# Linear attention and two expert layers in one kernel: the order of the stages, the shape of the attention products and the engine queues re-designed

## The chip, the cores and the metric

The kernel runs on one core of one Trainium2 chip. The metric is the device time of one execution in microseconds (us); the median of the runs before is 1416.45. The core has five engines with a queue each: TensorE (PE, matrix products; the loading of its stationary operand is listed apart as PEld), VectorE (DVE), ScalarE (ACT), GpSimd (POOL) and SyncE (SP, which here only issues transfers).

## The reference, cut to what matters

```python
def phi(x):                                   # q, k: (8 batches, 8 heads, 576 tokens, 64)
    proj = einsum('bhsd,df->bhsf', x, w_phi)  # 128 features
    proj = proj - max(abs(proj), axis=-1)
    return concatenate([exp(proj), exp(-proj)], -1)
q_p, k_p = phi(q), phi(k)
kv  = einsum('bhsf,bhsd->bhfd', k_p, v);  z = k_p.sum(2)
num = einsum('bhsf,bhfd->bhsd', q_p, kv)
den = einsum('bhsf,bhf->bhs', q_p, z)[..., None] + 1e-06
x = (num / den) -> (4608 tokens, 512)

h = x @ w_in                                  # 512 -> 1024; weights arrive as float64
e = exp(h - max(h));  solu = h * e / (sum(e) + 1e-9)
y = layernorm(solu) * g_ln @ w_out            # 1024 -> 512

logits = y @ w_gate + modality_bias[modality_id]   # 8 experts
e_idx = argmax(logits);  gate = softmax(logits)[e_idx]
out = gate * (relu(y @ w1[e_idx]) @ w2[e_idx])     # 512 -> 1024 -> 512
```

## The kernel before

The work has two parts. Class `P1` computes the attention and the first dense layer (`moe1`) for 36 tiles of 128 tokens and sends each token's place to a list of its expert. Class `P2` computes the chosen expert for slots of up to 256 tokens.

**Number formats.** Many products are made as three passes of a rounded format (`F32R`): high by high, high by low, low by high. The name ends in h or l. Where plain `F32` operands are multiplied, the trace shows two instructions, each with its own weight load, for one `matmul` of the code.

**The k side.** `k_fetch` brings one head's 512 rows (block of 64 x 512, twice on the 128 partitions; every ninth block holds the last 64 rows of all heads of a batch: 72 blocks). From block 18 on POOL splits a block into high and low halves. `k_phi` (L313) projects it, takes the largest magnitude of each row (DVE), and makes `exp(p-m)` and `exp(m-p)` on ACT in eight pieces of 128 columns, because the bias differs for each. `kv_head` (L363) multiplies the features of one head with `[v, 1]`: 8 products with 65 columns (16 instructions), two heads make a pair; `kM` adds the last 64 rows; `kE` copies the sums to `kvsb`, which holds two batches.

**The q side.** A unit `u` has 256 tokens of four heads (36 units). `q1` projects them transposed (feature on partition) into two PSUM banks that stay in use; DVE takes maxima over features by a transposing reduction; `q2` finishes them, splits them and sends them through two small transfers to two partitions (`mr`); `q3` subtracts them by one more product with `negones` and ACT makes the exponentials. `q_num` (L459) uses the q features as stationary operand, 128 tokens at a time:

```python
for sg in range(2):
    nc.tensor.matmul(o, qp[:, sg, h0 + h, tt*128:tt*128+128], kv[:, b % 2], start=(sg == 0), stop=(sg == 1))
```

Column 65 is the denominator; DVE divides. `x_T` turns each tile of x with four PE transposes and splits it.

**moe1.** `m_mm1` (L504) has 24 products of 512 columns, softmax and norm on ACT and DVE; `m_T` turns the result with 8 transposes; `m_mm2` (L556) has 48 products of 260 columns, the last 8 of which are the gate logits; `m_route` (L586) computes the place and POOL scatters it.

**The decoding of weights.** `prep_a` to `prep_e` turn 16 chunks of float64 weights into high and low parts, with passes over 128x512 elements on DVE, ACT and POOL, and 32 transposes and 32 small products on PE.

**The order.** All is interleaved: `PRO`, `LOOP`, `LOOP2`, `TAIL` are written-out lists of steps. `manual_schedule` fixes the order of PE (in `PRO` of SP too, in `TAIL` of POOL too); the other engines' orders are chosen by the planner.

```python
LOOP = "q3(u);lA(0);mT(t);kE();lA(1);num(u,0);q1(u+1);num(u,1);mm1(t+1);kV(0);kV(1);q2(u+1);mm2(t);xT(u);R(t-1);ql(u+2);kM()"
```

One round of `LOOP` handles one unit `u = t+4`, one tile `t` and one pair of heads of k; `LOOP2` is the same without k. `W(n)` in `PRO` are matmuls without use, 52 in all.

**The experts.** `star` picks the expert with most tokens so far and fetches its weights early; `T0`, `M1`, `M2` compute slot 0 while the last tiles are routed; `run` has the loop over further slots. The next expert's `w1` is split into high (ACT, `hi`) and low (DVE, `lo`) in four pieces after the present slot's first product, and PE waits (`sW`) for all four.

Of the kernel before, what the change touches and what calls it, by code (L numbers as in the profile page):

```python
# [17 lines left out]
KB = 2  # L18
QP = 512
KS = 4  # L20
KSBUF = 2
KRB = 3
KSB = 3
KOLD = 18
KAH = 2
VTB = 3
CWV = {0, 6, 13}
HV = {0, 3, 8, 9, 13, 14, 15}
HP_ = {4, 10, 13, 14}
QV = 4  # L30
LEAD = 4
HP = 1000
TF = 3
XB = 4
ENG = lambda E: {E.PE, E.SP}
PRO = """P();W(6);P();kA(0);P();kA(1);P();ql(1);P();kA(0);W(6);kV(0);kA(1);kV(1);P();kM();ql(0);kA(0);kV(0)
kE();kV(1);P();kA(1);kM();kA(0);P();kA(1);kV(0);q1(0);P();kV(1);W(14);q2(0);q1(1);kM();P();kV(0)
q3(0);P();kE();q2(1);kA(0);P();W(10);kA(1);kV(1);q3(1);P();kM();P();ql(2);kE();N(0);W(16);P();kE()
ql(3);P();kV(0);D(11);q1(2);kV(1);q2(2);P();D(8);kM();D(9);kA(0);P();F(8);P();kA(1);N(1);q1(3);kV(0)
D(12);q3(2);kV(1);kE();kM();P();q2(3);kA(0);kE();F(11);D(10);F(9);xT(1);kA(1);N(2);ql(4);B();q3(3)  # L40
kV(0);D(13);F(10);kV(1);q1(4);kM();N(3);ql(5);q2(4);kE();D(14);F(12);P();D(15);xT(3);F(14);kA(0)
q3(4);mm1(0);num(4,0);kA(1);kV(0);num(4,1);ql(6);F(13);q1(5);mT(0);F(15);kA(0);kV(1);q2(5);kM();q1(6)
kA(1);kE();mm2(0);kV(0);q3(5);mm1(1);R(0);q2(6);num(5,0);mm1(2);ql(7);kA(0);kV(1);mT(1);kM();ql(8)
num(5,1);q3(6);q1(7);mm2(1);kA(1);kV(0);num(6,0);num(6,1);xT(5);q2(7);kV(1);kE();mT(2);mm1(3);R(1)
mm2(2);kM()""".split("\n")
LOOP = """q3(u);lA(0);mT(t);kE();lA(1);num(u,0);q1(u+1);num(u,1);mm1(t+1);kV(0);kV(1);q2(u+1);mm2(t);xT(u)
R(t-1);ql(u+2);kM()""".split("\n")
LOOP2 = """q3(u);mT(t);kE();num(u,0);q1(u+1);num(u,1);mm1(t+1);kV(0);kV(1);q2(u+1);mm2(t);xT(u);R(t-1);ql(u+2)
kM()""".split("\n")
TAIL = """kE();q3(T-1);mm1(T-4);mm1(T-3);num(T-1,0);mT(T-5);num(T-1,1);mm2(T-5);mT(T-4);R(T-6);xT(T-1);mm2(T-4)  # L50
R(T-5);X();star();mm1(T-2);mm1(T-1);sy();mT(T-3);mm2(T-3);SP(0);R(T-4);mT(T-2);mm2(T-2);SP(1);mT(T-1)
T0();R(T-3);mm2(T-1);R(T-2);M1(0);R(T-1);t1();M1(1);M1(3);t2();t4();M1(2);M2(0,0);t3();M2(0,1);G1()
M2(1,0);T0(1);M2(1,1)""".split("\n")
# [3 lines left out]
def layout(inp):  # L57
# [3 lines left out]
    kt = np.empty((B, 9, 2, D, 512), np.float32)  # L61
    kt[:, 1:] = k[:, :, :512].transpose(0, 1, 3, 2)[:, :, None]
    kt[:, 0] = k[:, :, 512:].transpose(0, 3, 1, 2).reshape(B, 1, D, 512)
    o['kt'] = kt.reshape(B * 9, 128, 512)
# [8 lines left out]
    qt = q.transpose(1, 3, 0, 2).reshape(2, 4, D, 18, 256).transpose(3, 0, 2, 1, 4)  # L73
    qi = np.empty((18, 2, 2, D, 4, 256), np.float32)
    qi[:, :, 0] = qt
    qi[:, :, 1] = qt
    o['qi'] = qi.reshape(18, 2, 128, 1024)
# [31 lines left out]
class P1:  # L109
    def __init__(s, tc, A, y_dram, tk, ws, nchunk=18, dbg=None, stack=None, top=None):  # L110
# [3 lines left out]
        s.tc, s.nc, s.A, s.y, s.ws, s.nchunk = tc, tc.nc, A, y_dram, ws, nchunk  # L114
# [19 lines left out]
        s.nk = s.nf = 0  # L134
# [6 lines left out]
        s.x = {}  # L141
        s.qs, s.qst, s.qpt, s.e, s.pr, s.tp = {}, {}, {}, {}, {}, {}
# [3 lines left out]
        s.xT, s.z = {}, {}  # L146
        s.dbg = dbg

    def bank(s, name):
        return s.ps.tile([128, 512], F32, tag="b", name=name)  # L150

    def setup(s):
# [16 lines left out]
        nc.vector.memset(s.mhalf, -0.5)  # L169
        s.winl = s.wp.tile([128, 4, 1024], F32R, name="winl")  # L170
# [3 lines left out]
        s.wgt = c.tile([128, 4, 8], F32, name="wgt")  # L174
        s.cst = s.top.tile([128, 480], F32, name="cst_s")
# [30 lines left out]
    def prep_a(s, i):  # L206
# [1014 lines left out]
```

## Time and profile before

| | |
|---|---|
| three runs, us | median 1416.45, from 1411.86 to 1428.68 |
| profiled execution, from first to last instruction | 1438.4 us (no other time of it is given) |
| TensorE busy | 1382.6 us, 96% |
| VectorE / ScalarE / GpSimd busy | 744.3 / 566.7 / 446.0 us |
| mean granted TensorE clock | 0.963 |

"Busy" counts an instruction from its start to its modelled end, and TensorE instructions overlap; the difference between the starts of two groups in the timeline is the time that the first one really took. The clock of TensorE has two levels, 1.2 and 2.4 GHz, which a window row shows as 0.50 and 1.00; before the first change in the record it prints 1.00.

### The profile page before, as it was taken

How to read it: one execution, taken by the hardware profiler on the slowest of the kernel's cores; microseconds unless marked ns; L12 is line 12 of the kernel's file. 1: busy time of each engine (PE TensorE's matmuls, PEld its weight loads, DVE VectorE, ACT ScalarE, POOL GpSimd, SP SyncE). 2: the span in 40 equal slices, each digit the busy share in tenths (PEclk: the TensorE clock that was granted, in tenths of full speed). 3: DMA queues.
4: the chain of work that ended last, by engine and by line, in shares of the span. 5: the costliest groups of instructions: out<-in, count | busy, mean ns of one | idle time of the engine just before them, and what ended most of it. 6: DMA issues, size and time to landing. Idle time of an engine off the chain costs nothing. (4 is left out here: it accounts for less than half of the span.)

```text
span 1438.4 us, 24600 instructions
## 1 busy us (share of the span) xinstructions
PE 1382.6 (96%) x9100; PEld 1258.8 (88%) x9100; DVE 744.3 (52%) x2019; ACT 566.7 (39%) x1470; POOL 446.0 (31%) x454
## 2 busy tenths in 40 slices
PE   7999999999999999999999999889999999999994
PEld 7788979989989999999999889778998979999883
DVE  7773656676676666767676666651111142111143
ACT  4574444454354554555453323412222242222143
POOL 5562435343334444353532201222111121111121
PEclk9975999999999999999999999899999999999997
DMA  7241244244412433332311000314111132111132
GB/s 248 81 147 53 70 95 105 62 72 76 70 46 77 78 78 71 71 91 64 84 40 38 16 16 16 147 46 177 45 45 52 38 119 91 46 45 45 53 120 64
DMA packets 41740, 107.82 MB, mean 75 GB/s; under 512 B 10210, under 2 KB 10610, under 8 KB 40576
## 3 DMA queue, kind: packets, MB, share of 16 engines
q1 hardware_dynamic: 32832, 79.65, 20.7%
q0 software_dynamic: 8768, 26.30, 5.6%
q8 instruction: 87, 1.43, 0.5%
q14 instruction: 53, 0.43, 0.1%
HBM read 86.58 MB, written 20.63 MB: 75 GB/s over the span
## 5 line engine op out<-in xcount | busy, mean ns | idle before, releaser
L769 DVE SCALAR_TENSOR_TENSOR wol<-ph,woh 128x512 fp32r<-128x512 f32 x72 | 49.7, 691 | 308.2 <-ACT woh L765 308.2
L566 PE MATMUL y<-woh,zh 128*128 128x260 f32 x576 | 167.4, 291 | 3.5 <-ACT zh L552 3.5
L740 PE MATMUL ph<-yh,w1h 128*128 128x256 f32 x576 | 163.7, 284 | 4.8 <-issue 3.3
L566 PE MATMUL y<-woh,zl 128*128 128x260 f32 x576 | 164.1, 285 | 3.5 <-DVE zl L553 3.2
L566 PE MATMUL y<-wol,zh 128*128 128x260 f32 x576 | 164.6, 286 | 0.0
L740 PE MATMUL ph<-yl,w1h 128*128 128x256 f32 x576 | 163.5, 284 | 0.0
L740 PE MATMUL ph<-yh,w1l 128*128 128x256 f32 x576 | 162.3, 282 | 0.0
L475 PEld LDWEIGHTS num<-kvsb,qp_s 128*128 128x128 f32 x1152 | 144.3, 200 | 5.6 <-ACT qp_s L456 2.1
L475 PE MATMUL num<-kvsb,qp_s 128*128 128x65 f32 (+1 forms) x1152 | 145.8, 282 | 0.9 <-ACT qp_s L456 0.5
L378 PEld LDWEIGHTS kvps<-vt_s,kp_s 128*128 128x128 f32 x1024 | 136.0, 214 | 5.1 <-issue 1.6
L378 PE MATMUL kvps<-vt_s,kp_s 128*128 128x65 f32 x1024 | 136.2, 296 | 0.0
L754 PE MATMUL po<-winh,woh 128*128 128x512 f32 x312 | 124.7, 400 | 0.5 <-DVE wol L1173 0.5
L754 PE MATMUL po<-winh,wol 128*128 128x512 f32 x312 | 122.6, 393 | 0.0
L754 PE MATMUL po<-winl,woh 128*128 128x512 f32 x312 | 122.4, 392 | 0.0
L527 ACT ACTIVATE e_s<-h,nm 128x512 f32<-128x512 f32 x72 | 48.8, 683 | 186.2 <-DVE nm L521 186.2
L515 PE MATMUL h<-winh,xh 128*128 128x512 f32 x288 | 116.8, 406 | 0.0
L980 POOL DMA_INDIRECT yr<-ybuf,cidxi x42 | 44.1, 1050 | 230.9 <-ACT yh L758 204.4
L566 PEld LDWEIGHTS y<-woh,zh 128*128 128x128 f32 x576 | 110.3, 192 | 5.1 <-ACT zh L552 3.9
L740 PEld LDWEIGHTS ph<-yh,w1h 128*128 128x128 f32 x576 | 109.0, 189 | 6.2 <-issue 3.6
L566 PEld LDWEIGHTS y<-woh,zl 128*128 128x128 f32 x576 | 110.4, 192 | 4.0 <-DVE zl L553 3.5
L515 PE MATMUL h<-winh,xl 128*128 128x512 f32 x288 | 113.8, 395 | 0.0
L515 PE MATMUL h<-winl,xh 128*128 128x512 f32 x288 | 113.8, 395 | 0.0
(257 smaller groups left out, 3075.7 us busy)
## 6 DMA issues: line engine op xcount, KB each, us to landing
kr<-in_kt SPq DMA_DIRECT2D x72, 256.0 KB, 2.7
qt_s<-in_qi SPq DMA_DIRECT2D x36, 512.0 KB, 3.2
raw<-in_w SPq DMA_DIRECT2D x6, 2048.0 KB, 9.5
vt_s<-in_vi SPq DMA_DIRECT2D x32, 325.0 KB, 6.5
ybuf<-ysb SPq DMA_DIRECT2D x36, 256.5 KB, 4.5
raw<-in_win SPq DMA_DIRECT2D x8, 512.0 KB, 4.9
raw<-in_wout SPq DMA_DIRECT2D x8, 512.0 KB, 5.8
mr<-mh SPq DMA_DIRECT2D x72, 4.0 KB, 1.8
```

The costliest lines, as they stand in the source:

```text
L378: nc.tensor.matmul(pb[:, sg, a, :], kp[:, sg, c, :], vt[:, 4*a+c, :], start=(a == sg == c == 0), stop=False, skip_group_check=True)
L475: nc.tensor.matmul(o, qp[:, sg, h0 + h, tt*128:tt*128+128], kv.rearrange("p a d -> p (a d)") if two else kv[:, b % 2], start=(sg == 0), st ...
L515: nc.tensor.matmul(h[j], a[:, kk, :], w[:, kk, 512*j:512*j+512], start=(n == 0), stop=(n == 11))
L527: nc.scalar.activation(out=ej, in_=h[j], func=AF.Exp, bias=nm, accum_out=sums[:, j:j+1])
L566: nc.tensor.matmul(yb[j][:, 0:260], a[:, kk, :], w[:, kk, 260*j:260*j+260], start=(n == 0), stop=(n == 23))
L740: m = s.nc.tensor.matmul(ph[:, (f % 2)*256:(f % 2)*256 + 256], s.w1[w][:, k*1024 + f*128:k*1024 + f*128 + 128], x[:, k, :], start=(n == 0) ...
L754: m = s.nc.tensor.matmul(po, x[:, f*256 + h*128:f*256 + h*128 + 128], s.w2[w][:, f*512:f*512 + 512], start=(f == 0 and i == 0), stop=(f == ...
L769: return s.nc.vector.scalar_tensor_tensor(out=s.hl[:, o], in0=ph, scalar=0.0, in1=s.hh[:, o].bitcast(F32), op0=ALU.max, op1=ALU.subtract)
L980: G.indirect_dma_start(out=s.yr[j % 2][:, b, :], out_offset=None, in_=p.y, in_offset=bass.IndirectOffsetOnAxis(ap=idx[:, 2*j+b:2*j+b+1], a ...
```

## The change

The k side goes first. Blocks of k now hold two heads (one on each half of the partitions, 36 blocks in plain F32) and `k_proj` issues the two heads' products alternately. After 20 pairs of heads the units of q begin (`RAMP` mixes in the other 12 pairs), then the main loop has no k work but one last group. `kvsb` keeps the sums of all 8 batches. The weights' decoding (`prep`) has a lower priority in the planner than the features of k, and fewer of its passes are on DVE. Exponentials of k are made in two instructions of 512 columns after a subtraction on DVE; for heads 3, 5 and 7 in eight pieces as before.

A unit of q has 512 tokens of two heads. Its projection is one plain F32 product for each head; the maxima go to DRAM and come back as a broadcast over 128 partitions; DVE subtracts. Numerators come out transposed: the sums `kv` are stationary (64 columns for each head, `tile_position`), q features move. Denominators have a product of their own, with the column of sums repeated over 32 columns; they go to DRAM, back in another shape for the reciprocal, to DRAM and back as a broadcast; POOL multiplies. In `q_den` a unit has four blocks of 256 columns (a head and half of its tokens each), in every ninth unit 16 of 64; in `q_num` two of 512. The transposes of x go. Main loop and tail fix the order of all five engines.

In part two, PE waits for halves of the next expert's weights, whose high parts are made earlier; the entry into slot 0 has another order.

```diff
+HP_ = {0, 3, 4, 8, 10, 13, 14, 15}
+LEAD = 6
+RAMP = {-7: 2, -6: 2, -5: 2, -4: 2, -3: 2, -2: 1, -1: 1}
+NOPREP = {0, 3, 6, 9, 12, 15}
+KCHUNK = {3, 5, 7}
+LOOP = """q1(u+1);qa(u+1);nrm(t);yc(t-1);den(u);de(u);num(u);q2(u+1);qb(u+1);xc(u-1);ne(u);ra(t-1);mT(t);zz(t);qc(u+1);dr(u);rx(t-1)
+m1(t+1,0);mx(t+1,0);R(t-1);rb(t-1);rs(t-1);m1(t+1,1);mx(t+1,1);q3(u+1);ee(t+1);q4(u+1);dl(u);yo(t-1);ql(u+3);mm2(t);xm(u)"""
...
+    def prep_step(s):
+        if s.pi < 19:
+            with s.tc.high_priority(-60):
+                s.prep()
...
+    def k_proj(s):
+        sb = [s.bank("kps", "bq"[blk % 2 if blk < QFIRST else 0]).rearrange("p (c f) -> p c f", f=128) for a in range(2)]
+        for c in range(4):
+            for a in range(2):
+                o = slice(64*a, 64*a + 64)
+                nc.tensor.matmul(sb[a][:, c, :], ks[o, c*128:(c+1)*128], s.wphi[o, :], start=True, stop=True)
...
+        su = kp[:, 1]
+        nc.vector.tensor_tensor(out=su, in0=sb, in1=m[:, :, None].to_broadcast([128, 4, 128]), op=ALU.subtract)
+        nc.scalar.activation(out=kp[:, 0], in_=su, func=AF.Exp, scale=1.0)
+        nc.scalar.activation(out=kp[:, 1], in_=su, func=AF.Exp, scale=-1.0)
...
     def q1(s, u):
-            nc.tensor.matmul(pb, s.whh, rhs, start=True, stop=False)
-            nc.tensor.matmul(pb, s.wll, rhs, start=False, stop=True)
+            o = slice(64*j, 64*j + 64)
+            nc.tensor.matmul(pbs[j], s.wphi[o, :], qs[o, :], start=True, stop=True)
...
+    def qb(s, u):
+        nc.vector.tensor_reduce(out=m, in_=tp[0:32, 0:128].rearrange("p (q i) -> p i q", q=4), axis=AX.X, op=ALU.max)
+        nc.sync.dma_start(out=s.md[u:u+1, :].rearrange("o (a b) -> (o a) b", b=32), in_=m)
+    def qc(s, u):
+        nc.sync.dma_start(out=mb, in_=s.md[u:u+1, :].broadcast_to([128, 1024]))
     def q3(s, u):
-            nc.tensor.matmul(pb, s.negones, mr[:, 16*j:16*j+16, :].rearrange("p a b -> p (a b)"), start=False, stop=True, skip_group_check=True)
+            nc.vector.tensor_tensor(out=d, in0=pbs[j], in1=d, op=ALU.subtract)
...
+    def q_den(s, u):
+        for sg in range(2):
+            for n, (a, z, b, p, (h, c), o) in enumerate(s.blocks(u)):
+                g = 32*(2*a + z)
+                k = s.kv[:, p // 2, 2*(p % 2) + a, sg, b, 64:65].to_broadcast([128, 32])
+                nc.tensor.matmul(pb[g:g+32, o], k, qp[:, sg, h, c], start=(sg == 0 and n < 4), stop=(sg == 1), skip_group_check=True, tile_position=(0, g))
+    def d_out(s, u):
+        nc.scalar.activation(out=rd, in_=pb[:, 0:256], func=AF.Identity, bias=s.eps)
+        nc.sync.dma_start(out=s.dd[0][u], in_=rd[0:128:32, :])
+        nc.sync.dma_start(out=d8, in_=s.dd[0][u].rearrange("g (k e) -> (g k) e", e=8))
+    def d_rec(s, u):
+        nc.vector.reciprocal(out=r8, in_=d8)
+        nc.sync.dma_start(out=s.dd[1][u].rearrange("g (k e) -> (g k) e", e=8), in_=r8)
+    def d_in(s, u):
+        for a in range(2):
+            nc.sync.dma_start(out=rb[64*a:64*a+64], in_=s.dd[1][u:u+1, 2*a:2*a+2].rearrange("o z c -> o (z c)").broadcast_to([64, 512]))
...
+    def q_num(s, u):
+        for sg in range(2):
+            for n, (a, z, b, p, (h, c), o) in enumerate(s.blocks(u)):
...
+                else:
+                    c = o = slice(0, 512)
+                nc.tensor.matmul(pb[64*a:64*a+64, o], s.kv[:, p // 2, 2*(p % 2) + a, sg, b, 0:64], qp[:, sg, h, c], start=(sg == 0 and (n in (0, 2))), stop=(sg == 1), skip_group_check=True, tile_position=(0, 64*a))
...
+    def x_mul(s, u):
+        s.nc.gpsimd.tensor_tensor(out=x, in0=x, in1=rb, op=ALU.mult)
+    def x_split(s, u):
+        def both(h, l, x):
+            nc.scalar.copy(h, x)
+            nc.gpsimd.tensor_tensor(out=l, in0=x, in1=h.bitcast(F32), op=ALU.subtract)
-    def x_T(s, t):
-            nc.tensor.transpose(pb[:, kk*128:(kk+1)*128], x[:, kk*128:(kk+1)*128], s.ident)
...
+        with s.tc.manual_schedule(engines={PE}):
+            s.warm(14)
+            ramp = sum(RAMP.values())
+            for i in range(NPAIR - ramp):
+                s.kS()
+                if i == 0:
+                    s.warm(8)
+                    s.setup2()
...
+                if i not in NOPREP:
+                    s.prep_step()
...
+        with s.tc.manual_schedule(engines={PE, ET.DVE, ET.Activation, ET.SP, ET.Pool}):
+            for t in range(nu - LEAD + 1):
...
             def full(j):
                 for b in range(4):
+                    if b == 2:
+                        wait(0, j, 1)
                     s.t_mm1(ph[b], b).then_inc(sM1, 1)
```

In `LOOP` the letters stand for: q1 projection, qa/q2/qb/qc maxima, q3 subtraction, q4 exponentials, den/de/dr/dl denominators and their transfers, num/ne numerators, xm/xc multiply and split, m1/mx/ee/nrm/mT/zz/mm2/yc the steps of moe1, ra/rx/rs/yo/R/rb the gate, the store and the places.

## Rows read from the trace of the kernel before

**Rows 1.** Page, busy us (share of the span) and instructions of each engine.
```profile
PE 1382.6 (96%) x9100; PEld 1258.8 (88%) x9100; DVE 744.3 (52%) x2019; ACT 566.7 (39%) x1470; POOL 446.0 (31%) x454
```
**Rows 2.** Windows: length, busy PE, PEld, DVE, ACT, POOL (instructions), PEclk, DMA share, GB/s.
```profile
0.00:40.00 40.00, 32.17 (x134) 29.10 (x135) 31.35 (x48) 20.38 (x43) 21.60 (x22) 1.00 0.64 223
40.00:100.00 60.00, 56.30 (x271) 49.41 (x269) 43.46 (x69) 36.33 (x94) 31.49 (x23) 0.80 0.36 125
100.00:200.00 100.00, 97.84 (x579) 88.24 (x579) 55.51 (x161) 46.07 (x132) 34.42 (x32) 0.81 0.21 58
...
600.00:800.00 200.00, 200.00 (x1460) 185.18 (x1460) 136.11 (x422) 100.06 (x301) 74.57 (x83) 1.00 0.25 62
...
900.00:950.00 50.00, 42.64 (x287) 39.64 (x287) 34.39 (x122) 19.16 (x39) 12.77 (x12) 0.90 0.31 116
950.00:1000.00 50.00, 43.40 (x253) 37.93 (x252) 13.25 (x47) 8.21 (x16) 13.17 (x13) 0.93 0.41 144
...
1100.00:1200.00 100.00, 96.51 (x595) 86.94 (x594) 26.97 (x36) 29.10 (x49) 18.64 (x18) 0.98 0.26 87
...
1400.00:1439.00 39.00, 20.34 (x88) 16.00 (x87) 13.88 (x16) 13.50 (x19) 8.15 (x8) 0.78 0.24 78
```
**Rows 3.** Timeline of PE, one round of the steady loop: start, length, work.
```profile
703.83 0.48 PE L428 MATMUL qps<-qs_s,wcat 128*128 128x512 f32 x1
...
704.84 1.90 PE L475 MATMUL num<-kvsb,qp_s 128*128 128x65 f32 x16
706.55 0.48 PE L515 MATMUL h<-winh,xh 128*128 128x512 f32 x1
...
712.22 3.68 PE L378 MATMUL kvps<-vt_s,kp_s 128*128 128x65 f32 x32
...
715.77 0.37 PE L566 MATMUL y<-woh,zh 128*128 128x260 f32 x1
...
721.62 1.03 PE L495 MATMUL xTp<-ident,x_s 128*128 128x128 f32 x8
722.41 0.25 PE L593 MATMUL pos<-roh,tri 128*128 128x8 f32 x1
...
722.63 0.69 PE L388 MATMUL kvps<-vt_s,kp_s 128*128 128x130 f32 x4
723.26 0.73 PE L454 MATMUL qps<-mr,negones 2*128 2x512 f32 x2
```
**Rows 4.** Timeline of PE in the first 100 us.
```profile
24.98 3.67 PE L378 MATMUL kvps<-vt_s,kp_s 128*128 128x65 f32 x16
...
29.55 2.07 PE L322 MATMUL kps<-wphi_s,kr 64*128 64x128 f32 x8
...
41.74 3.09 PE L322 MATMUL kps<-wphi_s,kr 64*128 64x128 f32 x16
...
98.53 1.16 PE L322 MATMUL kps<-wphi_s,kr 64*128 64x128 f32 x8
```
**Rows 5.** Windows as in rows 2, two stretches of the start.
```profile
95.00:100.00 5.00, 5.00 (x43) 4.63 (x42) 4.94 (x8) 2.45 (x6) 1.29 (x1) 1.00 0.00 0
...
120.00:140.00 20.00, 20.00 (x90) 18.68 (x90) 5.21 (x18) 9.02 (x27) 4.98 (x5) 0.50 0.21 71
```
**Rows 6.** Groups by line and form: busy us, mean ns; idle before them, releaser.
```profile
L347 ACT ACTIVATE kp_s<-ksum,km 128x128 f32<-128x128 f32 x216 | 84.7, 392 | 0.0
...
L340 ACT ACTIVATE kp_s<-ksum 128x512 f32<-128x512 f32 x4 | 2.5, 626 | 1.8 <-PE kvps L378 0.9 <-DVE ksum L339 0.9
...
L332 DVE TENSOR_REDUCE km<-ksum 128x4 f32<-128x512 f32 x54 | 36.7, 679 | 0.6
...
L311 PE MATMUL warm<-winh,wcat 128*128 128x512 f32 x52 | 20.4, 561 | 4.4 <-DVE wcat L162 3.0 <-DVE qm L439 1.3
```
**Rows 7.** Page, DMA issues: KB each, median us to landing.
```profile
qt_s<-in_qi SPq DMA_DIRECT2D x36, 512.0 KB, 3.2
...
mr<-mh SPq DMA_DIRECT2D x72, 4.0 KB, 1.8
```

More of the change, by code (lines that the diff above doesn't have):

```diff
@@ L443, in q2 @@
-        mr = s.sm.tile([2, 32, 32], F32R, tag="mr", name="mr", bufs=1)
-        for z in range(2):
-            nc.sync.dma_start(out=mr[z:z+1].bitcast(F32), in_=mh[:, z, :].bitcast(F32))
-        s.qst[u] = (pbs, mr)
+        nc.sync.dma_start(out=s.md[u:u+1, :].rearrange("o (a b) -> (o a) b", b=32), in_=m)
+        s.qst[u] = pbs
+    def qc(s, u):
+        nc, pbs = s.nc, s.qst[u]
+        mb = s.qp.tile([128, 1024], F32, tag="mb", name="mb")
+        nc.sync.dma_start(out=mb, in_=s.md[u:u+1, :].broadcast_to([128, 1024]))
+        s.qst[u] = (pbs, mb)
@@ L560, in m_mm2 @@
         yb = [s.bank(f"y{j}") for j in range(2)]
-        ysb = s.mp.tile([128, ROW], F32, tag="ysb", name="ysb")
-        for j in range(2):
+        for j in order:
             n = 0
@@ L567, in m_mm2, with m_y, m_choose @@
                     n += 1
-        nc.scalar.copy(ysb[:, 0:260], yb[0][:, 0:260])
-        nc.scalar.copy(ysb[:, 260:512], yb[1][:, 0:252])
+        s.yb[t] = yb
+    def m_y(s, t, order=(0, 1)):
+        nc, yb = s.nc, s.yb[t]
+        ysb = s.mp.tile([128, ROW], F32, tag="ysb", name="ysb")
+        for j in order:
+            w = (260, 252)[j]
+            nc.scalar.copy(ysb[:, 260*j:260*j+w], yb[j][:, 0:w])
+        s.yb[t] = (yb, ysb)
+    def m_choose(s, t):
+        nc = s.nc
+        yb, ysb = s.yb.pop(t)
         T = lambda n, w=8, d=F32: s.sm.tile([128, w], d, tag=n, name=n, bufs=3)
@@ L623, in N @@
-        def N(u):
-            num(u, 0)
-            num(u, 1)
-        def xT(u):
-            if 0 <= u < nu and u % 2:
-                s.x_T(u - 1)
-                s.x_T(u)
-        E = mybir.EngineType
-        env = dict(kA=s.kA, kV=s.kv_head, kM=s.kM,  kE=s.kE, cum=cum, ql=ql, q1=q1, q2=q2, q3=q3, N=N, num=num, xT=xT, P=s.prep, D=s.prep_d, F=s.prep_e, W=s.warm, B=s.prep_bias, mm1=ok(s.m_mm1), mm2=ok(s.m_mm2), mT=ok(s.m_T), R=ok(s.m_route))
-        with s.tc.manual_schedule(engines=ENG(E)):
-            for x in PRO:
-                exec(x, env)
@@ L654, in build @@
             for x in TAIL:
-                for y in x.split(';'):
-                    with s.tc.high_priority(-HP if y.startswith('SP') else 0):
-                        exec(y, env)
+                do(x)
+YS = 128 * (36 - STAR)
 NS = 25
@@ L831, in tab1 @@
-        end = T("cend", 8)
+        next(place)
+        S8 = [128, 8, 8]
+        tmp = s.tmp = T("ctmp", 64).rearrange("p (a b) -> p a b", a=8)
+        st = s.st = T("cst2", 16).rearrange("p (a b) -> p a b", a=2)
+        V.tensor_tensor(out=tmp, in0=s.L, in1=pr[:, 0:1, :].to_broadcast(S8), op=ALU.mult)
+        next(place)
+        V.tensor_reduce(out=st[:, 0, :], in_=tmp, axis=AX.X, op=ALU.add)
+        next(place, None)
+        end = s.end = T("cend", 8)
         V.tensor_tensor(out=end, in0=st[:, 0, :], in1=nt, op=ALU.add)
@@ L1068, in pe @@
             def pe(j):
-                either(PE, j, full, half)
+                if j == 1:
+                    full(j)
+                    return
+                for x, f in zip(val[j % 2][1::-1], (full, half)):
+                    with PE.If(x > 0):
+                        f(j)
+                    PE.end_ifs()
             pe(1)
@@ L1195, in full @@
         tp = top.enter_context(tc.tile_pool(name="tabs", bufs=1))
-        p = P1(tc, i, y, tk, None, stack=top, top=tp)
+        md = dp.tile([36, 1024], F32, name="mdb")
+        dd = [dp.tile([36, 4, 256], F32, name=f"ddb{z}") for z in range(2)]
+        p = P1(tc, i, y, tk, md, dd, stack=top, top=tp)
         p2 = P2(tc, i, out, p, top)
```

748 lines of the change are left out of this document (423 added, 325 removed).

## The prediction

> **What bounds the kernel now.** I read the page first: TensorE is busy for 1382.6 of 1438.4 us, VectorE for half of that [rows 1]. Then the windows, to see whether that share is an average over stages: between 600 and 800 us PE is busy all 200 us at the full clock, so there only less PE work shortens the kernel; the start (the first 200 us), the passage from the first part to the experts (900 to 1000 us) and the end have waits and a lower clock [rows 2]. Last the timeline of PE in one round of the loop, where the difference of two starts is what a group really took, since a busy time counts overlapping tails twice [rows 3].
>
> By these differences one unit and one tile cost: q1 1.01 us (703.83 to 704.84), numerators 1.71 for half a unit, so 3.42, `mm1` 5.67, `mm2` 5.85, turning x 0.79 for two tiles, so 0.40, places 0.22, q3 some 0.73; `mT` has as many transposes as two tiles of x, 0.79. Together 18.1 us. One pair of heads of k adds 3.55 (712.22 to 715.77, 32 instructions, 0.111 each) and 0.63 for `kM` (722.63 to 723.26) and its projection [rows 3].
>
> The sum below is made against the profiled span, 1438.4 us. The runs' median, 1416.45, is 1.5% less; the result is scaled by that ratio at the end.
>
> **Units of q and tiles, 36 times.** Unchanged are `mm1`, `mm2`, `mT`, places: 5.67 + 5.85 + 0.79 + 0.22 = 12.5 us. The other 5.6 us go and three products in plain F32 come.
>
> No F32 product with 512 columns stands in the trace. Its two instructions cost from 0.236 us each (an `mm1` instruction: 5.67/24) to 0.44, if they grow in columns as 128 columns do (0.11 us: eight in 1.16 with the tail of the last) [rows 3, 4]. I take 0.44, since 128 F32 columns take nearly as long as the 260 of `mm2` (5.85/48 = 0.122), which looks like two passes [rows 3].
>
> New q1: two heads on the two halves of the rows. That such halves run side by side the trace shows: eight instructions of one head take 2.07 us, sixteen of two consecutive heads, which lie on opposite halves, 3.09 and not 4.1; they meet only where the blocks join [rows 4]. In the changed kernel they alternate from the start, so I count 2 x 0.44 = 0.9, and 0.2 for entering and leaving the mode (the eight at 98.53 took 0.27 more than 8 x 0.111, tail included) [rows 4]: 1.1 us.
>
> Denominators: 16 instructions of 256 columns on four groups of 32 array columns, 0.22 each; numerators: 8 of 512 on two groups of 64, 0.44 each. No group of columns is used in the trace. Bounds: one after another 3.5 + 3.5, and 0.4 for the modes, 7.4 us; all side by side 0.9 + 1.8 + 0.4 = 3.1. Between them: the two instructions of one product can't overlap each other, and if the next group starts only in program order, denominators take 9 steps of 0.22 and numerators 5 of 0.44, 4.6 us with the modes. The nearest row is that of the row halves, where the later block did begin beside the earlier one [rows 4], so I take 3.8, between the last two.
>
> A unit is then 12.5 + 1.1 + 3.8 = 17.4 instead of 18.1: 36 x -0.7 = **-25 us**; ends 36 x -1.4 = -50 and 36 x 0.1 = +4 with overlap; without any, 36 x 2.9 = +104, which is a rival below.
>
> The Trainium skill speaks against the better end: "TensorE: Matmul & The Clock Gate", Part 3, says that weight loads overlap running matmuls only when the row group differs, which column groups don't give, though it also lists three column groups at 2.38 times the speed of one. By the first rule the sum would take the 4.6 us and this term would be +4; no row here shows column groups.
>
> **The start and the k side.** The number of k-v products stays. The projection costs PE about what it did: per pair 16 instructions on two halves, 8 x 0.111 + 0.2 = 1.1 us. What changes is the company. Before, until about 50 us, PE ran back to back at the lower level: sixteen k-v instructions took 3.67 us against 1.8 later [rows 3, 4]; so it did from 120 to 140 us (clock 0.50 at 20.00 of 20 us busy) [rows 5], and the clock over 40 to 100 and 100 to 200 us was 0.80 and 0.81 [rows 2]. I count half of the 32 busy us before 40 as lost, 0.20 of 60 and 0.19 of 100 us in the next two windows, and 14 us of waits (7.8, 3.7 and 2.2 us not busy): 16 + 12 + 19 + 14 = 61 us [rows 2]. The changed kernel has a stage of 20 pairs with nothing but k and decoding. At the full clock a pair costs PE 36 x 0.111 + 1.1 + an eighth of a further projection = 5.2 us, the stage 104; at the lower level twice that, 208. ACT bounds it too: per batch (four pairs) nine sets of features, six in two instructions of 0.63 and three in eight of 0.39, 7.5 + 9.4 = 16.9 us or 4.2 a pair, some 0.4 for `kE`, a half pass, and of the decoding some 56 passes of 0.63 in all by the code, 14 of 16 chunks in this stage, 1.5 a pair: 6.1 us [rows 6]. DVE has less (0.68 a pass, 15 passes a batch, 2.6 a pair, and the decoding) [rows 6]. So PE would wait a little at the full clock, and would be the bound at the lower one. The rows show both: small F32 products alone didn't lift the clock from 120 to 140 us, and the same mix with a few wide ones kept it at 1.00 from 95 to 100 us, PE never idle [rows 5]. The 22 warm-up matmuls at the front and the extra k block after every eighth pair are the wide work here. I take 7 us a pair, 140 for the stage, 36 lost, and 6 for the first transfers: 42 against 61, and the twelve pairs of the ramp, which lie among wide products, lose nothing: **-19 us**, from -55 (nothing lost but the 6) to +49 (all at the lower level: 104 lost).
>
> Of 52 warm-up matmuls, 20.4 us of PE time [rows 6], 22 stay: -12, or 0 where they filled waits. I take **-10**.
>
> **The passage and the experts.** Between 900 and 1000 us PE isn't busy for 7.4 + 6.6 us and at 0.90 and 0.93 clock, which costs 5 + 3.5 [rows 2]: some 22 us lost. The new tail puts the split of weights and the tables of slots between the last tiles, and product halves of slot 0 between them, so I count half back, **-11**, bounds 0 and -22. From 1100 to 1200 us PE lacks 3.5 us, and of the 18.7 in the last 39 us some 12 lie behind the last store [rows 2]; weights made ready by halves and earlier can give back at most 3.5 + 7. I take **-6**, from -11 to 0. The slots themselves don't change.
>
> **The queues.** Fixed orders add waits. On SP a unit has md out, mb in, dd out, d8 in, r8 out and two rb in; each "in" waits at the head of the queue for the landing of its "out", and holds the next unit's transfers. A 4 KB transfer landed after 1.8 us, 512 KB after 3.2 [rows 7], so three pairs take some 3 x (1.8 + 2 to 3.2) = 11 to 15 us of a round of 17.4, which fits. The maxima must be back when `mm1` ends, some 10 us after they left: 5 to 7 us needed. After `mm1` DVE subtracts (2 x 0.68) and ACT makes four exponentials after the two of the tile: about 6 to 7 us until the next denominators, for which `mm2` and q1 give 5.85 + 1.1. This is the tightest place: I count **+5 us** in all, from 0 to 36 (one us each round). POOL gets a multiplication and a subtraction per unit in place of the k and q splits, and is not near its limit.
>
> **Sum.** -25 - 19 - 10 - 11 - 6 + 5 = -66, so 1372 against 1438.4, or 0.954 of it; 0.954 x 1416.45 = 1351. The k stage is the term of which I am least sure and its better half is as likely as the worse; TensorE's overlap of column groups is worth 25 us on the better side and 29 on the worse. I predict **1351**.
>
> **Rivals.** *Column groups don't overlap* (slower). 36 units at 7.4 instead of 3.8 us: +130 on the forecast's 1372, 1502, scaled 1479. Against it: the halves of rows overlap [rows 4]. It turns the result slower by 2% (1445, or 1467 against the span, 95 us over the forecast) from 2.6 us more in a unit, 6.4 us for both products. 12%.
>
> *Program order and cold k stage* (within 2%): products at 4.6 (+29), 20 pairs at the lower level (+68), waits of one us in each round (+31); two of them together +60 to +99, 1432 to 1471 against the span, 1410 to 1448 scaled; one of them and a part of another 1390 to 1410. For it: the stretch from 120 to 140 us [rows 5] and, by the trace so far, nothing that rules out any of the three. 19%.
>
> *All goes well*: side by side at once (-25), k stage at 5.5 us a pair (-30), the passage closed (-11): 1306 against the span, 1286 scaled. For it: PE kept the clock in the same mix [rows 5]. 14%.
>
> **How the numbers follow.** The forecast, 1305 to 1388, has 55%. Its range, most of the better rival's below and of the cold one's above give 1280 to 1430, which leaves out the 12% and some 7 on either end. Two per cent, 28 us, is about what a measurement tells from no change here, as the three runs spread by 17. Faster by over 2% (below 1388): 55 + 14 = 69%; within: 18%; slower (above 1445): 12% and the worst of the cold case, 13%.
>
> **What would show it.** Right: in a timeline of PE the numerators of a unit in 1.8 to 2.3 us and the denominators in 0.9 to 2.0, a round of 17 to 18 us without gaps before the denominators, the k stage at about 7 us a pair with a clock that changes level, the first slot of the experts some 60 us earlier. Wrong: numerators at 3.5; a round set by ACT's exponentials or by SP; k pairs at 10 us with the clock at 0.50; or a loop below 16.5 us, if one F32 instruction of 512 columns costs nearer to 0.236.

## The result and the profile after

The changed kernel takes 1301.7 us (median of 4 runs, 1299.5 to 1304.6) against 1416.5 (median of 3, 1411.9 to 1428.7) for the kernel before on the same chip: 0.918 of it, 95% interval 0.912 to 0.924. Times here and below are those of fast runs: an execution that is over 1.5% longer than the fastest of its kernel is left out. The forecast was 1351, 0.954 of before. The direction was right and the time lies inside the range of 1280 to 1430; the gain was under-estimated, 8.2% instead of 4.6%. The profiled execution took 1303.9 us, span 1301.9, against 1438.4, so 136.5 us have to be accounted for where the sum had 66. The medians are only 115 apart: the profiled execution of the kernel before is a long one, and some 20 of the 136.5 us are its excess, not the change (where they lie is read below, with the warm-ups).

The page after, busy time of each engine, against [rows 1]:

```profile
PE 1264.7 (97%) x9199; PEld 1070.0 (82%) x9199; DVE 703.5 (54%) x1700; ACT 531.5 (41%) x1214; POOL 327.0 (25%) x308
```

PE is as full as it was and is busy for 118 us less. Windows of the changed kernel (columns as in rows 2):

```profile
0.00:40.00 40.00, 36.58 (x328) 33.16 (x330) 30.83 (x56) 26.24 (x63) 15.63 (x20) 1.00 0.71 228
...
93.00:103.00 10.00, 10.00 (x60) 9.77 (x61) 3.71 (x8) 7.77 (x23) 2.56 (x2) 0.51 0.34 109
...
100.00:200.00 100.00, 97.79 (x897) 82.74 (x897) 59.92 (x115) 72.75 (x177) 30.34 (x25) 0.98 0.43 130
...
600.00:800.00 200.00, 198.81 (x1407) 161.36 (x1404) 150.18 (x435) 81.92 (x200) 56.10 (x53) 1.00 0.41 83
800.00:850.00 50.00, 45.12 (x320) 41.69 (x320) 34.05 (x130) 13.82 (x29) 10.74 (x12) 0.98 0.15 44
```

Against [rows 2] the start has its clock: 0.98 from 100 to 200 us where it was 0.81, with one stretch at the lower level, 93 to 103 us. The middle is as full as before. The passage to the experts is now 50 us with 4.9 us of waits and a clock of 0.98, where it was 100 us with 14 and 0.90 to 0.93.

The timeline of PE in a steady round, against [rows 3]:

```profile
530.57 1.13 PE L416 MATMUL qps<-qt_s,wphi_s 64*128 64x512 f32 x4
531.63 1.07 PE L479 MATMUL den<-qp_s,kvsb 128*32 128x256 f32 x16
532.63 1.94 PE L521 MATMUL num<-qp_s,kvsb 128*64 128x512 f32 x8
534.50 0.28 PE L429 MATMUL qmt<-ident,mt 128*32 128x128 f32 x1
534.62 1.04 PE L618 MATMUL zT<-ident,e_s 128*128 128x128 f32 x8
...
547.14 1.13 PE L416 MATMUL qps<-qt_s,wphi_s 64*128 64x512 f32 x4
```

By the starts: q1 1.06, denominators 1.00, numerators 1.87, the round 16.57 us. And the stage of k, against [rows 4] (the number in brackets is PE's idle time ahead of the group, and what ended it):

```profile
9.17 1.16 PE L318 MATMUL kps<-wphi_s,kr 64*128 64x128 f32 x16 [1.74 <-DMA kr<-in_kt]
...
28.52 1.16 PE L318 MATMUL kps<-wphi_s,kr 64*128 64x128 f32 x16
29.61 3.79 PE L377 MATMUL kvps<-vt_s,kp_s 128*128 128x65 f32 x32
...
33.83 1.16 PE L318 MATMUL kps<-wphi_s,kr 64*128 64x128 f32 x16
...
92.75 6.69 PE L377 MATMUL kvps<-vt_s,kp_s 128*128 128x65 f32 x32 [1.51 <-ACT kp_s L341]
...
126.83 1.13 PE L416 MATMUL qps<-qt_s,wphi_s 64*128 64x512 f32 x4
```

A pair takes 5.31 us (28.52 to 33.83), almost from the first on, and the first unit of q starts at 126.8 us. At 92.75 PE waited 1.51 us for exponentials, and the k-v products behind that wait took 6.69 us instead of 3.79.

### The profile page after: what moved, and what is told of

Its sections match the earlier page's. It is cut to its first block, busy times and chain, and to the rows that moved or that the text cites. A ratio compares the mean times of both kernels' runs of the same rounds, so it can differ in the third digit from the quotient of the medians.

```text
span 1301.9 us, 24182 instructions
## 1 busy us (share of the span) xinstructions
PE 1264.7 (97%) x9199; PEld 1070.0 (82%) x9199; DVE 703.5 (54%) x1700; ACT 531.5 (41%) x1214; POOL 327.0 (25%) x308
## 4 chain that ended last, share of the span: by engine, by line
PE 76%; DMA 8%; DVE 8%; issue 2%; ACT 2%; POOL 1%; SPq 0%; POOLq 0%; ACTq 0%; DVEq 0%
PE ph L900 15%; PE po L915 14%; PE y L640 13%; PE h L572 13%; PE kvps L377 5%; PE num L521 4%; DMA rb<-ddb 3%; PE qps L416 3%; PE den L479 2%; PE zT L618 2%; PE kps L318 1%; DMA mb<-mdb 1%; PE pT L892 1%; PE ph L908 1%; DVE km L326 1%
## 5 line engine op out<-in xcount | busy, mean ns | idle before, releaser
L377 PE MATMUL kvps<-vt_s,kp_s 128*128 128x65 f32 x1024 | 124.3, 281 | 3.1 <-ACT kp_s L341 3.1
L377 PEld LDWEIGHTS kvps<-vt_s,kp_s 128*128 128x128 f32 x1024 | 119.7, 196 | 8.0 <-ACT kp_s L341 3.9
L915 PE MATMUL po<-winh,woh 128*128 128x512 f32 x296 | 117.1, 396 | 1.6 <-DVE wol L1406 1.6
L915 PE MATMUL po<-winh,wol 128*128 128x512 f32 x296 | 115.4, 390 | 0.0
L915 PE MATMUL po<-winl,woh 128*128 128x512 f32 x296 | 115.2, 389 | 0.0
L900 PEld LDWEIGHTS ph<-yh,w1l 128*128 128x128 f32 x576 | 109.3, 190 | 0.6
L900 PEld LDWEIGHTS ph<-yl,w1h 128*128 128x128 f32 x576 | 109.6, 190 | 0.0
L640 PEld LDWEIGHTS y<-wol,zh 128*128 128x128 f32 x576 | 108.3, 188 | 1.3
L926 ACT ACTIVATE woh<-ph 128x512 fp32r<-128x512 f32 x68 | 40.8, 600 | 151.7 <-PE ph L900 151.7
L1373 ACT ACTIVATE ob<-po,gq 128x512 f32<-128x512 f32 x40 | 27.2, 687 | 168.2 <-PE po L915 168.2
```

Of the source, the lines that this page charges most:

```text
L377: nc.tensor.matmul(pb[:, sg, a, :], kp[:, sg, c, :], vt[:, 4*a+c, :], start=(a == sg == c == 0), stop=False, skip_group_check=True)
L640: nc.tensor.matmul(yb[j][:, 0:260], a[:, kk, :], w[:, kk, 260*j:260*j+260], start=(n == 0), stop=(n == 23))
L900: m = s.nc.tensor.matmul(ph[:, (f % 2)*256:(f % 2)*256 + 256], s.w1[w][:, k*1024 + f*128:k*1024 + f*128 + 128], x[:, k, :], start=(n == 0) ...
L915: m = s.nc.tensor.matmul(po, x[:, o*256 + h*128:o*256 + h*128 + 128], s.w2[w][:, f*512:f*512 + 512], start=(f == 0 and i == 0), stop=(f == ...
L926: return s.nc.scalar.activation(out=s.hh[:, 512*b:512*b + 512], in_=ph, func=AF.Relu)
L1373: A.activation(out=ob[j % 2][:, h, :], in_=po[h], func=AF.Copy, scale=s.gq[:, j % 4, h:h+1]).then_inc(sO, 1)
```

## The experiments

The changed kernel itself ran again on the chip of the experiments as their mark, twice.

> The changed kernel again, unchanged, as the mark for the three others on the same chip. Nothing is in dispute: 1299 to 1305 us as before, if the chip makes no difference; a result more than 10 us off would mean that the others are to be read only against this run.

Measured: 1301.2 us (1295.7 to 1304.4), ratio to before 0.914 (0.906 to 0.922).

> The changed kernel once more, unchanged, as the mark for the two others: 1299 to 1305 us by the runs so far.

Measured, with the last group of experiments: 1306.6 (1302.2 to 1320.4), 0.919 (0.913 to 0.926). Differences of under some 6 us between kernels are not told apart here.

**The order of the column groups (grouped).**

```diff
     def q_den(s, u):
-        for sg in range(2):
+        for g0 in range(0, 128, 32):
+          for sg in range(2):
...
+                if g != g0:
+                    continue
```

and likewise in `q_num` by its two groups of 64.

> The products of the denominators and of the numerators are issued group of columns by group of columns (both instructions of one accumulation and all its blocks, then the next group) instead of turning from group to group; the same products. Theory A (groups overlap only with their neighbour in program order, and two instructions of one group never do): the numerators go from 1.87 to some 3.5 us, the denominators from 1.00 to some 3 us, 36 rounds times 3.6 = +130, so about 1430. Theory B (the queue also looks ahead over instructions of the same group, as it seemed to do with row halves): numerators 2 to 2.8, denominators 1 to 2, +10 to +50, so 1312 to 1352. Theory C (the order of issue is indifferent): 0 to +5.

Measured: 1314.6 us, +13 on the mark. The timeline of PE in this kernel, one of the four units with blocks of 64 tokens and the ordinary one after it, then a unit with blocks of 64 tokens in the changed kernel:

```profile
520.30 3.18 PE L482 MATMUL den<-qp_s,kvsb 128*32 128x64 f32 x64
523.41 3.77 PE L527 MATMUL num<-qp_s,kvsb 128*64 128x64 f32 x64
527.10 0.29 PE L429 MATMUL qmt<-ident,mt 128*32 128x128 f32 x1
...
540.80 1.09 PE L482 MATMUL den<-qp_s,kvsb 128*32 128x256 f32 x16
541.82 1.94 PE L527 MATMUL num<-qp_s,kvsb 128*64 128x512 f32 x8
543.69 0.28 PE L429 MATMUL qmt<-ident,mt 128*32 128x128 f32 x1
```
```profile
514.84 1.10 PE L479 MATMUL den<-qp_s,kvsb 128*32 128x64 f32 x64
515.87 2.13 PE L521 MATMUL num<-qp_s,kvsb 128*64 128x64 f32 x64
517.94 0.28 PE L429 MATMUL qmt<-ident,mt 128*32 128x128 f32 x1
```

In an ordinary unit, where four instructions in a row go to one group, nothing is lost: 1.02 and 1.87 us, all groups side by side. In the units where 16 (denominators) or 32 (numerators) in a row go to one group, the products take 3.11 and 3.69 us instead of 1.03 and 2.07 in the changed kernel, which issues the same small blocks in turn. Four such units x 3.7 us make 15 us, against 13 measured. So theory B holds in 32 units and A in four, and the single records say where the line is: in the slow denominators the first instruction of the next group starts 6 ns after the thirteenth of sixteen of the group ahead, in the numerators 5 ns after the 29th of 32. I read from this that a group's next three instructions can wait without holding the others, and that a fourth holds the queue; runs of a length between four and sixteen were not tried.

**Denominators issued twice (den_twice).**

```diff
     def q_den(s, u):
-        for sg in range(2):
+        for sg in (0, 1, 0, 1):
```

> The denominators' products are issued twice in each unit (the second set starts over, so the result is the same): 1.00 us more PE work in each of 36 units, nothing else. Theory A (PE alone sets the round, the transfers and helpers have slack): 36 x 1.0 = +36, so about 1338, and the round goes from 16.55 to some 17.55. Rival (the round is set by the chain denominators, DRAM, reciprocal, DRAM, multiplication, split, or by the maxima, and PE has hidden slack): under +10, with the round near 16.6 and the idle time of PE smaller.

Measured: 1329.9 us, +28.7 on the mark. The timeline of PE in this kernel:

```profile
543.08 1.93 PE L479 MATMUL den<-qp_s,kvsb 128*32 128x256 f32 x32
544.95 1.94 PE L521 MATMUL num<-qp_s,kvsb 128*64 128x512 f32 x8
```

The second set costs 0.87 us, the steady round grew from 16.57 to 17.43, and 36 x 0.86 = 31. Theory A: what PE is given to do is the round; the chain over DRAM and the helpers have the slack.

**No warm-ups (no_warm).**

```diff
-            s.warm(14)
...
-                    s.warm(8)
```

> The 22 matmuls without use at the front (14 and 8) are left out. Theory A (they bring the clock to its upper level before the stage of k begins, and that stage alone, of short F32 products with waits, would stay at the lower level for long): a pair of heads takes up to 10 us instead of 5.3 at first, +50 to +100 over 20 pairs, so 1350 to 1400. Rival (the k products lift the clock by themselves within the first pairs, or the time of the warm-ups balances what they give): -5 to +15, so 1295 to 1317, and the granted clock is at 1.00 from some 20 us on.

Measured: 1312.6 us (1307.1 to 1317.9), +11 on the mark. PE at the start of this kernel:

```profile
21.14 2.08 PE L318 MATMUL kps<-wphi_s,kr 64*128 64x128 f32 x16
23.15 7.09 PE L377 MATMUL kvps<-vt_s,kp_s 128*128 128x65 f32 x32
...
31.14 2.08 PE L318 MATMUL kps<-wphi_s,kr 64*128 64x128 f32 x16
...
51.14 1.88 PE L318 MATMUL kps<-wphi_s,kr 64*128 64x128 f32 x16
52.95 3.79 PE L377 MATMUL kvps<-vt_s,kp_s 128*128 128x65 f32 x32
...
137.93 1.13 PE L416 MATMUL qps<-qt_s,wphi_s 64*128 64x512 f32 x4
```

The mechanism is theory A's, the size the rival's. Without warm-ups the pairs run at 10.0 us, at the lower level; but after some 41 us of these products without a gap (11.14 to some 52.7 us) the clock rose, and from then on a pair took 5.3. (The clock column can't show this: it prints 1.00 all along here, as it does before the first change in a record; the level is read from the 7.09 and 3.79 us.) The first unit of q starts at 137.9 instead of 124.8 us in the mark. So the warm-ups, some 7 us of PE time of which 5 lie beside the first transfers, bring 11 to 13 us, and not 50.

**Warm-ups alone, in the kernel before (before_warm).**

```diff
-PRO = """P();W(6);P();kA(0);...
+PRO = """W(14);P();W(6);P();kA(0);...
     def warm(s, n):
-                s.nc.tensor.matmul(pb, s.whh, s.wz, start=True, stop=True)
+                s.nc.tensor.matmul(pb, s.wz[:, 0:128], s.wz, start=True, stop=True)
```

> The kernel before, with 14 more matmuls without use at the very front, on a tile of zeros that needs no transfer, and nothing else of the change. Theory A (what the changed kernel gains at its start is the clock, lifted by the warm-ups while the first transfers are under way): the sixteen k-v instructions at 25 us take some 1.9 instead of 3.67 us and the start is 10 to 25 us shorter, so a ratio to before of 0.982 to 0.993. Rival (the clock falls again in the waits that follow, or wide products alone don't carry it: the order of stages is the cause): within 5 us of before, and 3.67 again at 25 us.

Measured: 1430.7 us in 11 runs, 1.001 of before (0.995 to 1.006). The timeline of PE in this kernel:

```profile
1.46 7.63 PE L311 MATMUL warm<-winh 128*128 128x512 f32 x20 [1.46 <-POOL winh L167]
...
19.89 2.00 PE L378 MATMUL kvps<-vt_s,kp_s 128*128 128x65 f32 x16
...
27.52 7.09 PE L378 MATMUL kvps<-vt_s,kp_s 128*128 128x65 f32 x32 [3.69 <-ACT kp_s L340]
```

The clock did come up, 2.00 us for sixteen k-v instructions. But at 27.5 us PE had waited 3.69 us for exponentials, and the next 32 took 7.09; from 60 to 80 us the granted clock is 0.50. The rival's size holds and its cause, the fall in the waits that follow; its sign (3.67 again at 25 us) didn't come, as the fall came later. In this kernel a lifted clock is worth nothing, because the order of the stages lets PE wait.

This trace also shows where the long execution of the kernel before lost its time. Here the whole span is 1415.5 us; the eighth unit of q starts at 186.3 us, in the kernel before at 209.2, and from there to the end both take the same 1229.2 us. As far as this trace may stand for a shorter execution of the kernel before, the excess of over 20 us lies in the first 209 us.

**Exponentials of k in eight pieces again (all_chunks), and in fewer (chunk57).**

```diff
-KCHUNK = {3, 5, 7}
+KCHUNK = {0, 1, 2, 3, 4, 5, 6, 7, 'h'}
```

> The exponentials of all nine sets of features of a batch, not of three, are made as before in eight pieces of 128 columns (eight bias values), so the subtraction on VectorE goes for the other six. ScalarE then has 9 x 8 x 0.39 = 28 us for four pairs, 7 us a pair, and with the copies and the decoding 8.5 to 9. Theory A (the pair of 5.3 us rests on the pair of wide exponentials; ScalarE becomes the bound): the 20 pairs take 66 to 75 us more, so 1368 to 1380 in all. Rival (VectorE, 90.9 of 101 us busy in that stage, is what PE waits for; giving it less work balances what ScalarE gets): under +15.

Measured: 1370.8 us (1367.1 to 1383.5), 0.963 of before (0.953 to 0.974), inside theory A's range. Windows of this kernel:

```profile
80.00:113.00 33.00, 33.00 (x172) 31.63 (x171) 10.29 (x24) 17.59 (x60) 7.16 (x7) 0.50 0.33 113
113.00:127.00 14.00, 14.00 (x73) 13.54 (x73) 7.21 (x11) 8.60 (x31) 2.59 (x2) 0.50 0.25 83
127.00:160.00 33.00, 24.55 (x209) 22.81 (x208) 15.62 (x28) 26.93 (x84) 15.37 (x12) 0.81 0.43 137
```

Only part of it is ScalarE's own time. From 80 to 127 us PE is busy without a gap at the lower level while ScalarE works 26 of 47 us: the clock fell at the waits ahead of it (ScalarE is 23.6 of 28 and 36.1 of 40 us busy from 12 to 80 us), and then PE is the slow one. By the timeline a pair takes 5.31 us at 38 to 59 us, even with the eight pieces, and 10.0 from 68 to 128 us; theory A's time came, its 8.5 to 9 us a pair did not. The first unit of q starts at 180.2 instead of 126.8 us. The exponentials in two wide instructions thus carry some 70 of the gain of 115 to 120 us, as long as the decoding lies in the same stage.

With `KCHUNK = {5, 7}`:

> Only two heads of eight, not three, have their exponentials made in eight pieces: per four pairs ScalarE has 1.9 us less and VectorE 0.7 us more. Theory A (ScalarE is what keeps PE waiting in the stage of k): the waits of PE there shrink from some 3 us and the dip of the clock behind them goes, -3 to -10. Rival (VectorE is later than ScalarE): the waits grow, 0 to +8.

Measured: 1306.4 us (1305.6 to 1323.8), 0.918 of before. Too near to the mark for a verdict; from 12 to 127 us PE waits 3.2 us instead of 3.3 and the clock is 0.94 instead of 0.96, so neither theory's change of the waits came.

**The planner's order in the main loop (free_engines).**

```diff
-        with s.tc.manual_schedule(engines={PE, ET.DVE, ET.Activation, ET.SP, ET.Pool}):
+        with s.tc.manual_schedule(engines={PE, ET.Pool}):
```

> In the main loop and the tail only TensorE and GpSimd have the written order; VectorE, ScalarE and SyncE are ordered by the planner, as most of them were before the change. Theory A (the written order of all engines carries part of the gain: on SyncE each returned transfer waits at the head of its queue, and a planner that doesn't know these times lets PE wait): +20 to +60, so 1320 to 1360. Rival (PE alone sets the round with slack on all others): within 5 us of 1301.

Measured: 1372.5 us (1366.9 to 1373.3), 0.959 of before (0.951 to 0.967): +71 on the mark, above theory A's upper end. The two ran on different chips; by the ratios to the kernel before on each, 0.959 against 0.914 and 0.919, it is 57 to 64. By the traces the 35 rounds take 48 us more, and the way from the last numerators to the second slot of the experts 18. The waits of PE between 12 and 700 us in this kernel (us in total, times, longest):

```profile
PE qmt L429 <- DVE rmx L659: 38.0, 21, 3.2
```

The rounds take 16.6 to 21.0 us instead of 16.57; PE's order is the same in both kernels. VectorE's timeline in one of these rounds shows why:

```profile
562.46 1.76 DVE L610 TENSOR_SCALAR e_s<-e_s,mv,va 128x1024 f32<-128x1024 f32 x1 [0.69 <-POOL va L605]
564.15 0.70 DVE L423 TRANSPOSE_TENSOR_REDUCE mt<-qps 128x16 f32<-128x512 f32 x1
564.78 0.12 DVE L658 TENSOR_TENSOR lg<-y,bsel 128x8 f32<-128x8 f32 x1
564.83 0.69 DVE L423 TRANSPOSE_TENSOR_REDUCE mt<-qps 128x16 f32<-128x512 f32 x1
```

The norm of the tile (L610) and a step of the choice of expert (L658) stand ahead of the maxima of q (L423), whose transpose PE takes next; in the written order both maxima come before the norm. The releaser named is a short instruction right behind the second maximum. So it is VectorE's order that shows in PE's waits, and not theory A's transfers on SyncE; but three engines were set free at once, and no run separates them.

**The priority of the decoding (prio_p60).** The lower priority, taken back to the normal one, gives the same order of instructions on every engine, so that part of the change neither costs nor brings anything. Raised instead:

```diff
-            with s.tc.high_priority(-60):
+            with s.tc.high_priority(60):
```

> The passes of the decoding get a higher priority than the features of k in the planner, instead of a lower one (that the lower one alone, taken back to an equal one, gives the very same order of instructions on every engine, is known from the built programs). Theory A (passes of 0.7 to 1.7 us that VectorE and ScalarE make ahead of maxima, differences and exponentials make PE wait, and a wait brings the clock down, as at 92.75 us in the changed kernel): more waits and dips in the first 125 us, +5 to +30. Rival (both engines have room enough for either order): within 5 us of 1301.

Measured: 1321.9 us (1308.9 to 1326.3), 0.929 of before (0.922 to 0.936) against the mark's 0.919. The profiled execution is the shortest of the five; its timeline shows what theory A expects, a wait for a difference and a pair at the lower level behind it:

```profile
60.48 1.31 PE L318 MATMUL kps<-wphi_s,kr 64*128 64x128 f32 x14 [1.29 <-DVE kp_s L340]
61.72 7.09 PE L377 MATMUL kvps<-vt_s,kp_s 128*128 128x65 f32 x32
```

Some 13 to 15 us slower, with intervals that overlap: likely, not settled.

**A way to the better kernel that didn't work (late_pass, dve_order).** VectorE in the changed kernel, ahead of the dip at 93 us:

```profile
87.08 1.74 DVE L233 SCALAR_TENSOR_TENSOR cw<-cxh,cw 128x512 f32<-128x512 f32 x1 [2.39 <-POOL cw L232]
88.75 1.49 DVE L220 TENSOR_SCALAR cxs<-cxs 128x512 int32<-128x512 int32 x1
90.16 1.28 DVE L326 TENSOR_REDUCE km<-kps 128x4 f32<-128x512 f32 x2
91.36 0.68 DVE L340 TENSOR_TENSOR kp_s<-kps,km 128x512 f32<-128x512 f32 x1
```

Two decoding passes, the first held 2.39 us by GpSimd, run ahead of the maxima and the difference for which PE waits at 92.75.

```diff
     def prep_b(s, i):
-        nc.vector.scalar_tensor_tensor(out=w, in0=sq, scalar=2.0**-30, in1=w, ...)
+        s.later = lambda: nc.vector.scalar_tensor_tensor(out=w, in0=sq, scalar=2.0**-30, in1=w, ...)
...
     def kA(s, a):
         s.k_phi((b, 2*pr + a), s.kpb[a])
+        if a == 0:
+            s.flush()
```

> The one decoding pass on VectorE that waits for a result of GpSimd (the masking of small values) is issued a pair's first maximum and difference later, where its operand is long there; nothing else. In the chain of the changed kernel this pass at 87 us held VectorE for 1.74 us, then another 1.41, ahead of the maximum, the difference and the exponentials for which PE waited 1.51 us at 92.75, and there the clock fell for 10 us. Theory A (that pass is the cause of the dip): no dip at 93 us, the k stage 3 to 8 us shorter, 1294 to 1299. Rival (VectorE's total work is the cause, 91 of 101 us busy, and another pass takes the place): within 3 us of 1301.

Measured: 1301.1 us (1295.3 to 1305.3) against the mark's 1306.6. VectorE has the same order there, the wait of 1.51 us and the dip stayed (6.05 us for the 32 instructions at 92.71): the planner put the pass back, so this run tells nothing of the theory. Then VectorE's order was written out for the stage of k:

```diff
-        with s.tc.manual_schedule(engines={PE}):
+        with s.tc.manual_schedule(engines={PE, mybir.EngineType.DVE}):
             s.warm(14)
...
+        with s.tc.manual_schedule(engines={PE}):
             for t in range(-1 - LEAD, 0):
```

> In late_pass the planner had put the moved pass of VectorE back into the same place, ahead of the features, so the dip at 93 us stayed. Here VectorE's order in the stage of k is written as well as TensorE's (maximum and difference of each head first, the passes of the decoding after the pair, the pass that waits for GpSimd after the next pair's first head). Theory A (the planner's order on VectorE costs the stage its waits and the dip): no wait above 0.5 us and no dip between 60 and 125 us, the first projection of q at 115 to 120 us instead of 125 to 127, 1293 to 1299. Rival (VectorE now waits at the head of its queue for transfers or GpSimd, with the features behind it): new waits of PE, the first projection at 126 us or later, 1301 to 1320.

Measured: 1307.9 us (1306.4 to 1319.1), 0.916 of before (0.911 to 0.920). Windows of this kernel (its profiled execution, 1317.3 us, is the longest of the six):

```profile
12.00:107.00 95.00, 92.65 (x916) 88.17 (x916) 73.63 (x130) 77.87 (x197) 42.65 (x33) 1.00 0.59 184
107.00:160.00 53.00, 48.10 (x255) 43.11 (x257) 29.66 (x51) 30.05 (x72) 27.47 (x23) 0.57 0.28 86
```

The timeline of PE where the first of these windows ends:

```profile
105.02 0.66 PE L396 MATMUL kvps<-vt_s,kp_s 128*128 128x130 f32 x4
107.38 0.67 PE L262 MATMUL wT<-ident,cw 128*128 128x128 f32 x4 [1.70 <-ACT cw L249]
107.98 2.08 PE L325 MATMUL kps<-wphi_s,kr 64*128 64x128 f32 x16
109.99 7.09 PE L386 MATMUL kvps<-vt_s,kp_s 128*128 128x65 f32 x32
...
117.98 2.07 PE L425 MATMUL qps<-qt_s,wphi_s 64*128 64x512 f32 x2
```

Both theories were right in turn. Up to 105 us there is no wait above 0.5 us and no dip, and the first projection of q starts at 118.0 us, as theory A has it. But the decoding now comes late: PE waits 1.70 us for a chunk that it has to turn, and most of the stretch from 107 to 160 us runs at the lower level. The gain of 8 us is given back there. No version tried beats the changed kernel beyond the spread.

## Why the prediction was right, and where it was too small

**Units.** The mechanism was right, q1 too (1.06 against 1.1). The term was mis-sized in the step "so I take 3.8, between the last two": denominators and numerators take 2.87 us, below even the lower bound of 3.1, as little time goes into entering the modes. A unit takes 16.57 instead of 18.1: 36 x 1.5 = -55, not -25. The rows of before had held the answer: sixteen projections of two heads took 3.09 instead of 4.1 us [rows 4], four instructions saved of sixteen. I read this as an overlap in program order only; grouped points at the rule behind it: up to three instructions of a busy group wait while others pass. The changed kernel turns from group to group, so none is held. The Trainium skill's rule that speaks for 4.6 us ("TensorE: Matmul & The Clock Gate", Part 3) isn't borne out for column groups by this trace: 16 instructions, each some 0.22 us behind the one ahead of it in its group, took 1.00 together. The F32 instruction of 512 columns, taken as 0.44 us, measured 0.43 (1.87 us for four, one behind the other, in each group).

**The stage of k.** The step that failed is "I take 7 us a pair". It took 5.31, the ideal 5.2, with one pair at the lower level. First q at 126.8 us instead of 146; some 23 us are lost instead of 42, so with 61 before about -38 instead of -19. no_warm and before_warm divide this: the warm-ups bring 11 to 13 us, and, as before_warm suggests, they do so because the stage behind them has almost no waits; all_chunks shows what waits would have cost there, some 70 us. The rival "cold k stage" was a real danger: it is what all_chunks is.

Two readings behind the 7 us were wrong. "DVE has less" than ACT: from 12 to 127 us VectorE is busy for 97.9 us and ScalarE for 93.6. And the stretch from 120 to 140 us in the kernel before wasn't small products alone: it holds transposes and a product with 512 columns (two instructions at 134.41 us). In no_warm the clock did rise among small F32 products alone, after 41 us; the sum's choice of 7 us between 5.2 and 10 was a guess between two levels, and it came out on the better side.

**Warm-ups** (-10): 52 took 20.4 us [rows 6], 22 take 7, -13. (The 23 us lost in the stage of k hold these 7 us too.) **Passage** (-11): 14 us of waits and 8 of clock in 100 us [rows 2] became 4.9 and 1, about -16; the first slot's work starts 138 us earlier, not 60, as most of the gain lies ahead of it. **Experts** (-6): from the second slot's first product to the end 462.4 us became 454.9, -7.5. For these two terms there is no run; they are read from the two traces alone.

**Queues** (+5): between 258 and 714 us 27 rounds are together 8 us above 27 x 16.57, and den_twice shows PE as the bound of a round. But the cover that made this cheap is the written order: free_engines puts the price of the planner's order at some 60 to 70 us, 48 of it in the loop, more than I had for the worst case (36).

**Sum.** -55 - 38 - 13 - 16 - 7.5 + 8 = -121.5 of -136.5. Some 15 us are not assigned; the 7 us of warm-ups counted twice and the last rounds of the kernel before without k, at 19.0 to 19.3 instead of 18.1 us, are part of that. And against the medians, 115 us apart, the terms of the start are some 20 us too large, as the execution they are taken from was long there. So the stage of k and the warm-ups together are worth some 30 to 40 us rather than 51 against an ordinary execution, as far as before_warm's trace stands for one. The prediction's scaling, from 1372 to 1351, took the excess as spread over all stages; if it lies in the start, the sum had it in the 61 us already, and these 21 us nearer to the result are luck.

The two rivals on the slower side didn't come: column groups overlap fully, which takes away the first and one condition of the second, and the k stage kept its clock, which takes away another. The case that all goes well (1286) is nearer to the result than the forecast (1351): this case, given 14%, is in the main what happened.

**Open.** Not every wait brings the clock down: 1.01 us at 69.43 and 1.74 us at 9.17 in the changed kernel didn't, 1.51 at 92.75 did, and so did 1.29 at 60.48 in prio_p60. What tells them apart was not tried, nor what ends a stretch at the lower level: with the same products and no gap it lasted some 10 us in the changed kernel, 41 in no_warm and 60 in all_chunks (68 to 128 us).

## What to carry to other kernels

Small products on different row or column groups run side by side if the order turns from group to group; 16 and 32 instructions in a row to one group took most of that away here, four in a row nothing. A stage of short products is worth what its waits leave of the clock: first feed it (order of VectorE and ScalarE, fewer wide passes), then lift the clock ahead of it, for the second alone brought nothing in the kernel before. And where PE is the bound, look for the other engines' order too: here the written order of loop and tail was worth some 60 to 70 us with not one product changed.

## What the runs showed of the hardware that I had not expected

Four column groups of 32 start 6 to 7 ns apart and run as if each were alone; a queue passes over up to three waiting instructions of a busy group (13th of 16, 29th of 32). In no_warm the clock rose after 41 us in which PE ran nothing but short F32 products, without a gap; in all_chunks 60 us of them without a gap stayed at the lower level, and in the kernel before 20 us of short products, transposes and one product of 512 columns stayed at 0.50 [rows 5].
